# Experts sorted by their token counts, with a last large block each: 512 tokens for four experts and 448 for the other four

## The chip, the cores and the metric

The kernel runs on one core of a Trainium2 chip. The metric is the device time of one execution in microseconds (us); a version's time is the median of its runs. The core's engines are TensorE (PE in the profile; PEld is its weight loads), VectorE (DVE), ScalarE (ACT), GpSimd (POOL) and SyncE (SP), each with an instruction queue of its own, beside the DMA engines.

## The reference

Two parts run one after the other, all in float32. First an attention without softmax over 8 batches of 2496 tokens; then each token goes through the two-layer network of one of eight experts, which is chosen by a hash of the token's id.

```python
# u, v: (8, 2496, 256); z: (8, 2496, 64)
scores = (1.0 / S) * np.matmul(z, z.transpose(0, 2, 1))
attn = np.maximum(scores, 0.0) ** 2
x = (u * np.matmul(attn, v)).reshape(19968, 256)
# w1: (8, 256, 1024); w2: (8, 1024, 256)
expert_idx = token_ids * 2654435761 % 8
for e in range(8):
    mask = expert_idx == e
    out[mask] = np.maximum(x[mask] @ w1[e], 0.0) @ w2[e]
```

The multiplier is 1 modulo 8, so a token's expert is the low three bits of its id. How many tokens an expert gets depends on the ids alone; the kernel learns it only while it runs, so the program must hold for any distribution.

## The kernel before

**Attention.** 200 steps, one for each batch, group of 256 queries (per half of the sequence) and group of keys. TensorE makes scores (L251), ScalarE applies the relu and the square, VectorE forms sums and differences (L275 to L278), and TensorE multiplies them with v in seven products in place of eight (L326). The last query group of a half has 224 queries, so its matmuls have 224 columns. The order of all instructions is written out by hand.

**Routing.** The generator `places()` (from L433) computes, while the attention runs, the slot of each token in a DRAM buffer `x_slots`. The attention's loop calls it once in each step of the list ROUTE, up to its next `yield`; when it has ended, the gated rows of the attention are scattered to their slots by indirect DMAs of POOL (`sort`, L411), and the slots' token numbers are entered into a table (`enter`, L662). Inside `places()`:

- each token's expert (`eid`), a mask of 8 experts by 160 columns, and the number of tokens of each expert;
- a relabelling: the expert with the most tokens becomes label 0, by an exclusive or with its number (`most_i`), so that the others change places in pairs (L513 to L530);
- ranks by matmuls with triangular and full matrices and a scan (L543 to L550);
- `share()` (L560 on): a number of blocks for each label, by a shift of its count, a running sum, and a clamp of the sum at the number of blocks that there are;
- two levels, large blocks of 512 and small blocks of 128. A label gets a further large block if over 128 tokens are left. What doesn't fit goes to small blocks;
- zeros written by indirect DMAs into the last large and the last small block of each label (L653), and the expert of each block (`eb_i`), to be read by SP when it loads weights;
- the slot of each token, from its rank plus an offset by level (L630 to L650).

**Experts.** 40 large blocks (NL) of 512 tokens follow, five for each expert, one after another in the order of their slots. For a block, `load_x` fetches x in a layout that VectorE turns by transposes of 32 by 32 (`turn_x`, L753); `load_w` reads the expert's number from `eb_i` and fetches weights of 1.75 MB for each of the two layers, prepared beforehand as seven factors (`w_blocks`); `up_big` and `down_big` multiply, seven products in place of eight, with half a block's tokens (256) as the columns of each matmul (L972, L1011); the outputs are turned back through DRAM (L1027, L1029) and scattered to the output's rows (`store`, L924). The last large block takes `down_last`, which has the tokens as rows of the result. Up-projections, down-projections and transposes of neighbouring blocks are interleaved by the strings ORDER.

One small block (SMALLS = 1) is unrolled beside the last large block: `up_small` (L1067), `down_small` (L1078). Any further small blocks run in a loop at the very end (L1130), whose number of passes, `n_others`, is read from SBUF when the program gets there:

```python
    n_others = nc.values_load(others_i[0:1, 0:1], min_val=0, max_val=NR - SMALLS)
    with tc.For_i(0, n_others, 1) as n:
```

A pass reads the block's expert, loads both layers' weights (1 MB each), 128 tokens' x and 128 row numbers (`to`), turns x, does 16 and 8 matmuls in the source (32 and 16 instructions, since each float32 matmul is two in the trace), and scatters 128 rows.

Of the kernel before, what the change touches and what calls it, by code (L numbers as in the profile page):

```python
# [12 lines left out]
I32 = mybir.dt.int32  # L13
# [11 lines left out]
def kernel(  # L25
# [31 lines left out]
    NL = E * -(-N // (E * BLK))  # L57
    SMALLS = 1
    NR = max(E, (N - (NL - E) * BLK - E * (P + 1) + E * (P - 1)) // P)
# [361 lines left out]

# [10 lines left out]
    def places():  # L432

        with tc.tile_pool(name="route", bufs=1) as route:
# [15 lines left out]
            zero = route.tile([P, TB * D], F32)  # L450
# [13 lines left out]
            row_of = route.tile([P, 2], F32)  # L464
            nc.gpsimd.iota(row_of[:], pattern=[[NL * BLK, 2]], base=0, channel_multiplier=1,
                           allow_small_or_imprecise_dtypes=True)

            unused = list(range((NL - E) * TB, NL * TB + SMALLS, 7))

            def fill():  # L470
                if unused:
                    c = unused.pop(0)
                    n = min(7, NL * TB + SMALLS - c)
                    nc.sync.dma_start(
                        x_dram[ds(c * P, n * P), :].rearrange("(c p) d -> p c d", p=P), zero[:, 0:D].unsqueeze(1).to_broadcast([P, n, D]))
# [13 lines left out]

            def masks():  # L490
                c = 2 * (B - 1) * T
                nc.vector.tensor_copy(eid[:, 0:c], eid_i[:, 0:2 * (B - 1)].rearrange("p b t -> p (b t)"))
                for ts_ in (slice(0, 2 * LATE), slice(2 * LATE, T)):
                    n = ts_.stop - ts_.start
                    nc.vector.tensor_copy(eid[:, c:c + 2 * n].rearrange("p (b t) -> p b t", b=2), eid_i[:, 2 * (B - 1):, ts_])
                    c += 2 * n
                nc.vector.tensor_tensor(
                    mask[:], eid[:].unsqueeze(1).to_broadcast([P, E, C]),
                    iota_e[:].unsqueeze(2).to_broadcast([P, E, C]), op=OP.is_equal)
# [3 lines left out]
            yield  # L503

# [11 lines left out]
            most = route.tile([P, 1], F32)  # L516
            nc.vector.tensor_reduce(most[:], total[:], axis=AX.X, op=OP.max)
            nc.vector.tensor_scalar(total[:], total[:], most[:], float(-E), op0=OP.is_ge, op1=OP.mult)
            nc.vector.tensor_add(total[:], total[:], iota_e[:])
            nc.vector.tensor_reduce(most[:], total[:], axis=AX.X, op=OP.min)  # L520
            most_i = route.tile([P, 1], I32)
            nc.vector.tensor_copy(most_i[:], most[:])
# [3 lines left out]
            for n, cols in columns:  # L526
                x = eid_i[0:n, :, cols]
                nc.vector.tensor_tensor(x, x, most_i[0:n].unsqueeze(2).to_broadcast(list(x.shape)), op=OP.bitwise_xor)
                nc.vector.tensor_scalar(x, x, E - 1, None, op0=OP.bitwise_and)
# [45 lines left out]
            levels, base, added, unfilled = [], 0, None, []  # L575
            for size, spare, limit, name in ((BLK, BLK - P - 1, NL, "large"), (P, P - 1, NR, "small")):
                n, end = share(count, size, spare, limit, name)
                if limit == NL:
                    yield
                more = route.tile([P, E], F32, name=name + "_more")  # L580
                nc.vector.tensor_sub(more[:], end[:], n[:])
                nc.vector.tensor_scalar(more[:], more[:], float(size), float(base), op0=OP.mult, op1=OP.add)
                nc.vector.tensor_sub(more[:], more[:], first[:])
                total_more = route.tile([P, E], F32, name=name + "_total")
                nc.vector.tensor_copy(total_more[:], more[:])
                if added is not None:
                    nc.vector.tensor_sub(more[:], more[:], added[:])
                added = total_more
                levels.append((first, more, end))
                taken = route.tile([P, E], F32, name=name + "_taken")  # L590
                nc.vector.tensor_scalar(taken[:], n[:], float(size), None, op0=OP.mult)
                nc.vector.tensor_sub(count[:], count[:], taken[:])


                last = route.tile([P, E], F32, name=name + "_last")
                rows_i = route.tile([P, E], I32, name=name + "_rows")
                nc.vector.tensor_scalar(last[:], end[:], -1.0, 0.0, op0=OP.add, op1=OP.max)
                which = int(limit == NR)
                nc.vector.tensor_scalar(rows_i[:], last[:], float(P), row_of[:, which:which + 1], op0=OP.mult, op1=OP.add)
                unfilled += [(rows_i[:, e:e + 1], size // P) for e in range(E)]  # L600
                if limit != NR:
                    nc.vector.tensor_scalar(count[:], count[:], 0.0, None, op0=OP.max)
                    next_first = route.tile([P, E], F32, name=name + "_first")
                    nc.vector.tensor_add(next_first[:], first[:], taken[:])
                    first = next_first
                base += limit * size
                yield
# [3 lines left out]
            for (_, _, end), b0, nb in zip(levels, (0, NL), (NL, NR)):  # L611
                over = upto[0:1].rearrange(flat_e)[:, 0:nb * E].rearrange('p (j e) -> p j e', e=E)
                nc.vector.tensor_tensor(
                    over, end[0:1, :].unsqueeze(1).to_broadcast([1, nb, E]),
                    iota_b[:, 0:nb].unsqueeze(2).to_broadcast([1, nb, E]), op=OP.is_le)
                eb = route.tile([1, max(NL, NR)], F32, name="eb")
                nc.vector.tensor_reduce(eb[:, 0:nb], over, axis=AX.X, op=OP.add)
                nc.vector.tensor_scalar(eb_i[:, b0:b0 + nb], eb[:, 0:nb], float(E - 1), None, op0=OP.min)
                if nb == NL:
                    yield  # L620
            nc.vector.tensor_scalar(others_i[:], levels[1][2][0:1, E - 1:E], float(-SMALLS), 0.0, op0=OP.add, op1=OP.max)
            nc.vector.tensor_tensor(eb_i[:], eb_i[:], most_i[0:1].to_broadcast([1, NB]), op=OP.bitwise_xor)
            nc.vector.tensor_scalar(eb_i[:], eb_i[:], E - 1, None, op0=OP.bitwise_and)

# [4 lines left out]
            lowest, more, _ = levels[1]  # L629
            nc.vector.tensor_tensor(upto, rank[:], each(lowest), op=OP.is_ge)  # L630
            yield
            nc.vector.tensor_mul(upto, upto, each(more))
            for k in range(0, len(unfilled), 4):
                yield
                for rows, n in unfilled[k:k + 4]:
                    zeros(rows, zero, n)
            nc.vector.tensor_add(rank[:], rank[:], each(levels[0][1]))
            yield
            nc.vector.tensor_add(rank[:], rank[:], upto)
            yield  # L640
# [11 lines left out]
    def zeros(rows, zero, n):  # L652
        nc.gpsimd.indirect_dma_start(  # L653
            out=x_dram.rearrange("(r n) d -> r (n d)", n=n), out_offset=bass.IndirectOffsetOnAxis(ap=rows, axis=0),
            in_=zero[:, 0:n * D], in_offset=None, bounds_check=NS * P // n - 1, oob_is_err=False)
# [76 lines left out]

    def half(j):
        return len(slot_tiles(j)) * P // 2

    def load_x(j):
        n = len(slot_tiles(j)) * P
# [184 lines left out]
    def store(j, t, o):  # L922
        col = slot_tiles(j)[t]
        st = nc.gpsimd.indirect_dma_start(  # L924
            out=out[:], out_offset=bass.IndirectOffsetOnAxis(ap=idx[:, col:col + 1], axis=0),
            in_=o, in_offset=None, bounds_check=N - 1, oob_is_err=False)
# [75 lines left out]
    def down_big(j):  # L1002


        take, banks = down_factors(j), {}

        def made(m, _):
            ps, first = down_bank(m, banks)
            x, k = take[m]
            for f in range(FQ):  # L1010
                nc.tensor.matmul(ps[:], w2_block(w2[j], k)[:, f], x[:, f], start=first and f == 0, stop=f == FQ - 1, skip_group_check=True)  # L1011
            return ps[:]
        r = rpool.tile([P, 2, 2 * P], F32, name="ro")
        o = rpool.tile([P, 2, 2, 2 * P], F32, name="oT")
# [3 lines left out]
        def done(x, i, k, ps=None):  # L1018
            if ps is not None:
                nc.scalar.copy(x, ps)  # L1020
            elif i != k:
                for k in range(2):
                    nc.vector.transpose(y[:, ts(i, BLK // L // 2), :, k], o[:, k, i].rearrange("p (j r) -> p j r", r=L))
        yield from products(made, r[:, 0], r[:, 1], c(0, 0), c(0, 1), c(1, 0), c(1, 1), done)
        rows = nc.dram_tensor(f"o_{j}", (BLK, D), F32)
        for q in range(P // L):
            nc.gpsimd.dma_start(out=rows.rearrange("(j r) (q e) -> q r j e", r=L, q=P // L)[q], in_=y[ts(q, L)].rearrange("r j d k -> r j (d k)"))  # L1027
        y = rpool.tile([P, TB, D], F32, name="o_sb", bufs=1)
        nc.gpsimd.dma_start(out=y[:], in_=rows.rearrange("(t p) d -> p t d", p=P))  # L1029
# [61 lines left out]
    BIG, SMALL = list(range(NL)), [[]] * (NL - 1) + [list(range(NL, NL + SMALLS))]  # L1091
    assert SMALLS == 1
# [94 lines left out]
```

## Time and profile before

| | |
|---|---|
| median of 3 runs | 2441.69 us (2438.97 to 2443.9) |
| profiled execution | 2438.23 us |
| its span in the profile | 2436.4 us |
| mean granted TensorE clock | 0.998 |
| TensorE busy | 2416.5 us, 99% |
| VectorE, ScalarE, POOL busy | 1817.1, 728.1, 707.9 us |
| DMA | 559.59 MB, mean 230 GB/s |

In the lines of the profile, a group of instructions is given by its line in the kernel, engine, operation, output and inputs, shape and number; busy time in all and the mean of one in ns follow. In the timeline each line has the start and the duration in us and then the same names, with "x8" for eight instructions drawn together; what stands in brackets is idle time before and what ended it. A line of waits says who waited for whom, the total, how many times, and the longest. A line of windows gives a stretch, its length, the busy time of PE, PEld, DVE, ACT and POOL, the granted clock of TensorE, the DMA engines' busy share and GB/s.

Matmuls are pipelined, so the distance between the starts of two of them, not the duration of one, says what a matmul takes of TensorE's time.

### The profile page before, as it was taken

How to read it: one execution, taken by the hardware profiler on the slowest of the kernel's cores; microseconds unless marked ns; L12 is line 12 of the kernel's file. 1: busy time of each engine (PE TensorE's matmuls, PEld its weight loads, DVE VectorE, ACT ScalarE, POOL GpSimd, SP SyncE). 2: the span in 40 equal slices, each digit the busy share in tenths (PEclk: the TensorE clock that was granted, in tenths of full speed). 3: DMA queues.
4: the chain of work that ended last, by engine and by line, in shares of the span. 5: the costliest groups of instructions: out<-in, count | busy, mean ns of one | idle time of the engine just before them, and what ended most of it. 6: DMA issues, size and time to landing. Idle time of an engine off the chain costs nothing. (4 is left out here: it accounts for less than half of the span.)

```text
span 2436.4 us, 32657 instructions
## 1 busy us (share of the span) xinstructions
PE 2416.5 (99%) x11167; PEld 2010.0 (82%) x11167; DVE 1817.1 (75%) x3811; ACT 728.1 (30%) x1210; POOL 707.9 (29%) x742
## 2 busy tenths in 40 slices
PE   8999999999999999999999999999999999999998
PEld 6787787787787787787787788888888888888887
DVE  7778778868869769768778667777777777777774
ACT  4324314314324224224224212222222222222221
POOL 0002013433434424513411121333233323232323
PEclk9999999999999999999999999999999999999999
DMA  7766667888888888778778677777767776867683
GB/s 151 200 204 190 154 199 230 243 274 257 240 265 254 254 258 255 243 215 249 247 220 257 187 236 230 224 255 222 260 213 265 216 259 218 259 217 258 223 270 117
DMA packets 425193, 559.59 MB, mean 230 GB/s; under 512 B 257372, under 2 KB 350381, under 8 KB 406592
## 3 DMA queue, kind: packets, MB, share of 16 engines
q1 hardware_dynamic: 350704, 326.23, 47.6%
q0 software_dynamic: 41872, 133.39, 15.6%
q10 hardware_dynamic: 32448, 97.86, 12.1%
q8 instruction: 88, 1.44, 0.2%
q14 instruction: 81, 0.66, 0.1%
HBM read 353.28 MB, written 200.26 MB: 227 GB/s over the span
## 5 line engine op out<-in xcount | busy, mean ns | idle before, releaser
L255 ACT ACTIVATE a<-s_ps 128x512 f32<-128x512 f32 (+1 forms) x480 | 246.2, 599 | 699.2 <-PE s_ps L251 601.3
L326 PE MATMUL acc<-t,vc 128*128 128x256 f32 (+3 forms) x1600 | 402.2, 373 | 0.0
L326 PEld LDWEIGHTS acc<-a,v_sb 128*128 128x128 f32 (+1 forms) x1600 | 293.2, 190 | 119.1 <-issue 56.5
L411 POOL DMA_INDIRECT x_slots<-x_row,row x160 | 193.5, 1209 | 680.4 <-DVE x_row L389 558.4
L326 PE MATMUL acc<-a,v_sb 128*128 128x256 f32 (+3 forms) x1600 | 382.7, 382 | 0.1
L326 PE MATMUL acc<-t,v_sb 128*128 128x256 f32 (+3 forms) x1600 | 369.7, 373 | 0.0
L326 PEld LDWEIGHTS acc<-t,vc 128*128 128x128 f32 (+1 forms) x1600 | 303.5, 190 | 33.6
L326 PEld LDWEIGHTS acc<-t,v_sb 128*128 128x128 f32 (+1 forms) x1600 | 303.4, 190 | 33.6
L972 PE MATMUL h_ps<-xs,w 128*128 128x256 f32 x1280 | 316.0, 380 | 0.0
L1011 PE MATMUL o_ps<-h,w 128*128 128x256 f32 x1248 | 294.8, 379 | 0.0
L275 DVE TENSOR_TENSOR t<-a 128x512 f32<-128x512 f32 (+1 forms) x200 | 134.2, 671 | 203.9 <-ACT a L264 144.7
L979 ACT ACTIVATE h<-h 128x512 f32<-128x512 f32 x240 | 151.1, 630 | 418.6 <-DVE h L942 176.9
L972 PEld LDWEIGHTS h_ps<-xs,w 128*128 128x128 f32 x1280 | 243.6, 190 | 32.4
L1011 PEld LDWEIGHTS o_ps<-h,w 128*128 128x128 f32 x1248 | 243.1, 195 | 27.2
L251 PE MATMUL s_ps<-zT 64*128 64x512 f32 (+1 forms) x960 | 240.2, 616 | 7.8 <-DVE zT L186 7.8
L972 PE MATMUL h_ps<-xT,w 128*128 128x256 f32 x960 | 234.7, 380 | 2.5 <-DVE h L942 2.5
L1011 PE MATMUL o_ps<-hs,w 128*128 128x256 f32 x936 | 221.1, 379 | 0.0
L291 DVE STREAM_TRANSPOSE mirror<-a 128x256 f32<-128x256 f32 x640 | 217.8, 407 | 2.0 <-DMA scores<-mirror 1.8
L924 POOL DMA_INDIRECT out_dram<-o_sb,idx x156 | 159.3, 1021 | 187.4 <-DMA o_sb<-o 151.7
L662 POOL DMA_INDIRECT slot_tokens<-token,addr x160 | 171.1, 1069 | 134.7 <-DVE addr L650 86.3
L972 PEld LDWEIGHTS h_ps<-xT,w 128*128 128x128 f32 x960 | 182.7, 191 | 27.4 <-DVE h L942 2.9
L326 PE MATMUL acc<-a,vc 128*128 128x256 f32 (+3 forms) x800 | 201.1, 373 | 0.0
(182 smaller groups left out, 2610.1 us busy)
## 6 DMA issues: line engine op xcount, KB each, us to landing
w<-w_blocks SPq DMA_DIRECT2D x80, 1792.0 KB
scores<-mirror SPq DMA_DIRECT2D x192, 256.0 KB
a<-scores ACTq DMA_DIRECT2D x48, 1024.0 KB
scores<-mirror SPq DMA_DIRECT2D x224, 128.0 KB
a<-scores ACTq DMA_DIRECT2D x32, 896.0 KB
w_blocks<-w POOLq DMA_DIRECT2D x16, 1792.0 KB
xq<-x_slots SPq DMA_DIRECT2D x160, 128.0 KB
o<-y POOLq DMA_DIRECT2D x156, 128.0 KB
```

The lines of the kernel that those rows point to most:

```text
L251: nc.tensor.matmul(flat(ps)[:, 0:2 * w].rearrange("p (q c) -> p q c", q=2), tile_of_keys(b, h, s, j), q_h, start=True, stop=True)
L255: nc.scalar.activation(of[:, :, j, h].rearrange("p m q e -> p q m e"), flat(ps)[:, 0:2 * w].rearrange("p (q m e) -> p q m e", q=2, e=in_bl ...
L275: nc.vector.tensor_sub(t1, y12, y11)
L291: nc.vector.transpose(to, in_blocks(a, g)[:, :, j, h].rearrange("p i q (r t) -> p t i q r", t=2)[:, t])
L326: nc.tensor.matmul(acc[k][:, half, 0:w], x[0:n, j, :], y[0:n, j], start=(first and j == 0 and half == 0), stop=(last and j == 1), skip_gro ...
L411: st = nc.gpsimd.indirect_dma_start(out=x_dram[:, :], out_offset=bass.IndirectOffsetOnAxis(ap=row[0:m, c:c + 1], axis=0), in_=x_sb[0:m, q, ...
L662: st = nc.gpsimd.indirect_dma_start(out=slot_dram[:, None], out_offset=bass.IndirectOffsetOnAxis(ap=addr[0:n, to:to + 1], axis=0), in_=tok ...
L924: st = nc.gpsimd.indirect_dma_start(out=out[:], out_offset=bass.IndirectOffsetOnAxis(ap=idx[:, col:col + 1], axis=0), in_=o, in_offset=Non ...
L972: nc.tensor.matmul(ps[:, r], w1[j][:, k, ts(f + r, P)], y, start=first and r == 0, stop=True, skip_group_check=True)
L979: lambda o, i, k, ps=None: nc.scalar.activation(o, o if ps is None else ps, AF.Relu))
L1011: nc.tensor.matmul(ps[:], w2_block(w2[j], k)[:, f], x[:, f], start=first and f == 0, stop=f == FQ - 1, skip_group_check=True)
```

## The change

There are still 40 large blocks, but the first 32 (FULL) are shared out as full blocks, and the other eight are one "last" block for each label. The labels are now the experts' places in the order of their counts, the most first: each expert's label is the number of experts with more tokens. The last blocks of labels 0 to 3 hold up to 512 tokens, those of labels 4 to 7 up to 448. What is left beyond the last block goes to small blocks, of which there are now up to 28 in place of 27.

```diff
-    NL = E * -(-N // (E * BLK))
+    LASTS = (BLK,) * (E // 2) + (BLK - 2 * L,) * (E // 2)
+    FULL = E * (N // (E * BLK))
+    NL = FULL + E
     SMALLS = 1
-    NR = max(E, (N - (NL - E) * BLK - E * (P + 1) + E * (P - 1)) // P)
+    NR = max(E, -(-(N - FULL * BLK) // P))
```

The relabelling is a comparison of all pairs of counts, and the tokens' labels are read off the mask:

```diff
-            nc.vector.tensor_reduce(most[:], total[:], axis=AX.X, op=OP.max)
...
+            nc.vector.scalar_tensor_tensor(total[:], total[:], float(E), iota_e[:], op0=OP.mult, op1=OP.subtract)
+            nc.vector.tensor_tensor(pairs[:], *a_b(total[:], total[:]), op=OP.is_lt)
+            nc.vector.tensor_reduce(label[:], pairs[:], axis=AX.X, op=OP.add)
...
+            nc.vector.tensor_tensor(mask[:], mask[:], label[:].unsqueeze(2).to_broadcast([P, E, C]), op=OP.mult)
+            yield
+            labels = route.tile([P, C], F32)
+            nc.vector.tensor_reduce(labels[:], mask[:].rearrange("p e c -> p c e"), axis=AX.X, op=OP.add)
+            nc.vector.tensor_scalar(eid[:], eid[:], float(E), float(E), op0=OP.is_ge, op1=OP.mult)
+            nc.vector.tensor_add(eid[:], eid[:], labels[:])
             masks()
```

The levels become three. The shift of the large level now has no allowance (it was 383, so that over 128 left tokens made a block), and its clamp is FULL; `size_of` holds LASTS:

```diff
-            for size, spare, limit, name in ((BLK, BLK - P - 1, NL, "large"), (P, P - 1, NR, "small")):
+            for size, spare, limit, name in ((BLK, 0, FULL, "large"), (P, P - 1, NR, "small")):
+                if limit == NR:
+                    more = route.tile([P, E], F32, name="last_more")
+                    nc.vector.tensor_scalar(more[:], iota_e[:], float(BLK), float(FULL * BLK), op0=OP.mult, op1=OP.add)
+                    level(more)
+                    taken = route.tile([P, E], F32, name="last_taken")
+                    nc.vector.tensor_tensor(taken[:], count[:], size_of[:], op=OP.min)
+                    nc.vector.tensor_sub(count[:], count[:], taken[:])
...
                 n, end = share(count, size, spare, limit, name)
...
-            nc.vector.tensor_tensor(upto, rank[:], each(lowest), op=OP.is_ge)
-            yield
-            nc.vector.tensor_mul(upto, upto, each(more))
...
+            for k in (1, 2):
+                nc.vector.tensor_tensor(upto, rank[:], each(levels[k][0]), op=OP.is_ge)
+                yield
+                nc.vector.tensor_mul(upto, upto, each(levels[k][1]))
+                for e in range(4 * k - 4, 4 * k):
+                    zeros(rows_i[:, e:e + 1], zero)
+                yield
+                nc.vector.tensor_add(rank[:], rank[:], upto)
+                yield
```

The experts of the blocks (`eb_i`) are looked up from the labels by a comparison and a sum over eight. The indirect writes of zeros are now for small blocks alone, eight in place of sixteen; all last blocks are still zeroed beforehand by `fill()`. `places()` has 29 yields in place of 25.

In the expert part a block's matmuls, sums, loads and stores follow its number of tokens, and the last blocks are put among the full ones, the fewest tokens' first:

```diff
+    def tokens(j):
+        return BLK if j < FULL else LASTS[j - FULL] if big(j) else P
+
     def half(j):
-        return len(slot_tiles(j)) * P // 2
+        return tokens(j) // 2
...
-        nc.gpsimd.dma_start(out=y[:], in_=rows.rearrange("(t p) d -> p t d", p=P))
+        whole, rest = divmod(2 * n, P)
+        nc.gpsimd.dma_start(out=y[:, 0:whole], in_=rows[0:whole * P].rearrange("(t p) d -> p t d", p=P))
+        if rest:
+            nc.gpsimd.dma_start(out=y[0:rest, whole], in_=rows[whole * P:2 * n])
...
-    BIG, SMALL = list(range(NL)), [[]] * (NL - 1) + [list(range(NL, NL + SMALLS))]
+    BIG, SMALL = [x for e in range(E) for x in (*range(e * FULL // E, (e + 1) * FULL // E), NL - 1 - e)], [[]] * (NL - 1) + [list(range(NL, NL + SMALLS))]
```

The last large block of the order, which takes `down_last`, is that of label 0. The loop at the end is unchanged.

## The prediction

> **What bounds the kernel now.** I read the page first, then the waits, then the two stretches the change touches: a large expert block, and the end.
>
> ```profile
> span 2436.4 us, 32657 instructions
> ...
> PE 2416.5 (99%) x11167; PEld 2010.0 (82%) x11167; DVE 1817.1 (75%) x3811; ACT 728.1 (30%) x1210; POOL 707.9 (29%) x742
> ```
>
> ```profile
> PE s_ps L251 <- DVE zT L186: 7.8, 2, 6.9
> PE h_ps L972 <- DVE h L942: 2.5, 1, 2.5
> PE o_ps L1043 <- DVE ro L936: 0.6, 1, 0.6
> ```
>
> The three lines below the page's are all that TensorE (PE) waits for: 10.9 us. So the time is the number of matmuls times their spacing, plus a short tail. Only two things can matter: columns taken out of matmuls, and work put where TensorE no longer covers it.
>
> **How many blocks of which kind.** This is exact, from the inputs: with seed 0, token id modulo 8 gives the experts 2506, 2446, 2582, 2478, 2498, 2473, 2434 and 2551 tokens. Before, an expert takes a further large block if over 128 tokens are left; that makes 5 for each, 40 in all, and 22 tokens of the largest expert go to one small block. That one is unrolled (SMALLS = 1), so the loop at L1130 runs zero times. The trace agrees: 32 matmuls at L1067 are one small block.
>
> After, the full blocks are count // 512, running sum clamped to FULL = 32. In sorted order (2582, 2551, 2506, 2498, 2478, 2473, 2446, 2434) that is 5, 4, 4, 4, 4, 4, 4, 4 = 33, so the clamp leaves the last expert 3. The largest then has 22 tokens left, for which it occupies a "last" block of 512. The smallest has 2434 − 1536 = 898 left; its last block takes 448, and 450 remain: four small blocks. One is unrolled, **three go through the loop at the end**, which has no other work beside it.
>
> **Gain: four blocks of 448.** A 448-token block issues the same matmuls with 224 columns in place of 256. The attention part already runs both widths, in two stretches of 28 matmuls of equal make:
>
> ```profile
> 323.07 1.89 PE L326 MATMUL acc<-a,v_sb 128*128 128x256 f32 x8
> ...
> 329.11 1.90 PE L326 MATMUL acc<-a,v_sb 128*128 128x256 f32 x8
> ...
> 348.42 1.68 PE L326 MATMUL acc<-a,v_sb 128*128 128x224 f32 x8
> ...
> 353.72 1.68 PE L326 MATMUL acc<-a,v_sb 128*128 128x224 f32 x8
> ```
>
> The starts give 6.04 us / 28 = 0.2157 us at 256 columns and 5.30 / 28 = 0.1893 at 224. A block has (1280 + 960) / 40 = 56 matmul instructions up and 56 down: 112 × 0.2157 = 24.16 us, and the weight issues of SyncE (SP) below come 24.17 apart, so a block is matmul spacing and nothing else. Saved: 112 × 0.0264 = 2.96 us per block, **11.8 us** for four. VectorE is busy 691 of 964 us in these blocks (17.3 us per block), fits into the 21.2 us that remain, and shrinks too. The next block's transfers keep the DMA engines near 9 tenths for some 4.5 slices of 3.9 us, 17.7 us in each 24.17, and fit as well: their slack is 6.5 us a block, above the 2.96 that go.
>
> ```profile
> 2310.15 1.59 SPq L769 DMA_DIRECT2D w<-w_blocks  x2
> ...
> 2334.33 1.49 SPq L769 DMA_DIRECT2D w<-w_blocks  x2
> ```
>
> **Cost: three passes of the loop.** A pass loads 2 MB of weights and 128 KB of x, turns x, computes, and stores, one after the other: the weight tiles are single (bufs=1), and TensorE has nothing else. Its rows:
>
> ```profile
> 2359.80 0.41 SPq L772 DMA_DIRECT2D w1s<-in_moe_w_dram  x1
> 2361.01 21.13 SPq L769 DMA_DIRECT2D w<-w_blocks  x2
> ...
> 2383.34 1.95 PE L1067 MATMUL h_ps<-xTs,w1s 128*128 128x128 f32 x16
> ...
> 2416.67 0.78 POOL L1029 DMA_DIRECT2D o_sb<-o  x1 [2.90 <-issue]
> ...
> 2421.03 1.04 POOL L924 DMA_INDIRECT out_dram<-o_sb,idx  x1 [3.57 <-DMA o_sb<-o]
> ...
> 2424.04 3.62 PE L1078 MATMUL o_ps<-w2s,h 128*128 128x256 f32 x16
> ...
> 2431.36 0.97 POOL L924 DMA_INDIRECT out_dram<-o,idx  x1 [0.30 <-issue]
> ```
>
> - Loading, issue: 1.3 us from one weight load to the next on SP (2359.80 to 2361.01, and its register read).
> - Loading, transfer: 2.23 MB. Quickest: 424 GB/s, the best slice of the DMA view from 2280 to 2437 us, 5.3 us. Dearest: the 512 KB of o_sb landed 4.36 us after its issue began; less 0.78 of issue and 1.85 of landing that is 1.8 us, or 295 GB/s, hence 7.6 us. I take 6.4. Landing: 1.85 us, from the end of the last store's issue (2432.33) to SP's last semaphore of L1130 (2434.2). x is issued behind both weights, so TensorE waits for all of it.
> - Turning x: 0.44 (the one transpose of xTs) and a hand-over, 0.5 us.
> - Computing: up 2 × (1.95 + 0.68 for the relu), in turn since they share one PSUM tile; down 3.62; copy 0.37; some 0.9, an estimate, for the hand-overs (from the down matmuls' end, 2427.66, to ScalarE's copy, 2428.14, is 0.48; I count it as about two of them): 10.2 us.
> - Storing: 0.97 of issue and 1.85 of landing, 2.8 us.
> - From pass to pass: the engines must meet. At zero passes they already do, once; L1130's semaphores and branches end on SP at 2434.2 and on PE at 2434.8, 0.6 us. The program's end, which drains, clears semaphores and meets twice, takes 1.9 us (L1182, 2434.4 to 2436.3). I take 1.9, the nearer in kind.
> - TensorE's clock. It idles some 15 us in each pass, and the last matmul here ended at 2427.7:
>
> ```profile
> 2428.00:2429.00 1.00, 0.00 (x0) 0.00 (x0) 0.00 (x0) 0.37 (x1) 0.69 (x2) 1.00 0.11 37
> 2429.00:2430.00 1.00, 0.00 (x0) 0.00 (x0) 0.00 (x0) 0.00 (x0) 0.77 (x1) 0.88 0.44 148
> 2430.00:2432.00 2.00, 0.00 (x0) 0.00 (x0) 0.00 (x0) 0.00 (x0) 1.62 (x2) 0.50 0.27 91
> ```
>
> The column before the last two is the granted clock: 1.00, then 0.88, then 0.50, so it halves about 2 us after the last matmul and each pass starts at half. Half all the way doubles the streaming, 2 × 1.8 + 3.45 = 7 us (16 × 0.113 twice, 16 × 0.2157); recovery at once costs 0. The trace shows no recovery; I take the middle, 3.5.
>
> A pass: 1.3 + 6.4 + 1.85 + 0.5 + 10.2 + 2.8 + 1.9 + 3.5 = **28.4 us**; with the low ends of transfer, meeting and clock 22.5, with the high ends 33.1. Three: **85 us**, between 67 and 99.
>
> The Trainium skill, "TensorE: Matmul & The Clock Gate", Part 1, says that the clock falls to half after an idle window of about 3.4 us and returns after some 3.4 us of sustained work. The fall agrees with the row above; the return no row here shows. By it the first 3.4 us of matmuls run at half speed, an estimate of 1.7 us per pass in place of 3.5, and three passes would cost 80 us.
>
> **What costs nothing.** Routing grows by some 10 us of VectorE in steps of 0.2 to 2.3 us: two more passes over 1280 elements for the labels (1.49 as L497, 2.33 as L645), three more over rank (1.45 each, as L630 to L637), and small ones. From 320 to 600 us VectorE idles 57 of 280 while TensorE idles 0.02; that slack hides it. Uncovered it is 10 us; I put 0, and 10 into the range. Four more yields end routing some five steps (of about 7 us) later; sorting starts then, and its backlog of one more group is worked off by the seven fetches per 25 steps, against five made. Eight indirect zero fills go from POOL (about 1.1 us each, 9 us off a queue at 29%). A 448 block adds one POOL issue (0.78 us) ahead of its stores, hidden under 21 us of matmuls. The new order moves no load past another: every block fetched its own weights already.
>
> **Sum** against the profiled execution (2438.2 us, span 2436.4): 2438.2 − 11.8 + 85.2 = 2511.6. The median of the runs shown (2441.7) is 3.5 above that execution, so on its scale **2515 us**.
>
> **Rivals.**
> - *Three passes as above*, 22.5 to 33.1 us each: 2497 to 2529. Chance 0.72.
> - *Dearer passes*, 34 to 42 us: the loop body's instructions, which no engine has run here, arrive late (the page lists instruction transfers, q8 and q14), or 128 scattered 4-byte reads (`to`) land last. For it: nothing in the trace shows the body. Against: every piece of it has a row. 2532 to 2556. Chance 0.12.
> - *Cheaper passes*, 17 to 22.5 us: the next pass's weights start while the last one stores (2.8 + 1.9 us hidden), and the clock recovers at once. Against: L1130 has every engine meet. 2481 to 2497. Chance 0.12.
> - *No pass, faster*: the fifth full block of the largest expert doesn't displace one of the smallest, so that only the 448-blocks tell: 2441.7 − 11.8 = 2430. It decides from a largest expert under 2560 tokens on, or a pass under 11.8 / 3 = 3.9 us; but its matmuls alone stream for 7 us, and 2582 is counted. Chance 0.04: it is also the case that I misread the sharing.
>
> **The numbers.** The range 2487 to 2540 reaches from the middle of the cheaper case through the likeliest with 10 us for routing, into the dearer one. The measurement tells 0.2% (5 us) from no change: faster 0.04, same 0.01, slower 0.95.
>
> **What would show it.** three times the 32 + 16 matmuls of a small block, on the loop's own lines, in the final 85 us; matmuls of 128x224 in the expert part at 0.189 us spacing; blocks 21.2 us apart four times; the granted clock at 0.5 when each pass starts; TensorE idle before the loop still about 11 us. It would be wrong if the loop ran another number of times, or if TensorE waits appeared in attention, where routing grew.

## The result and the profile after

The changed kernel takes 2511.16 us (median of 4 runs, 2507.2 to 2517.55); the kernel before, measured beside it, 2442.8. The ratio is 1.0285, with a 95% interval of 1.0269 to 1.0301: slower, 4 us under the predicted 2515. The profiled execution took 2513.03 us, with a span of 2511.2, 74.8 more than before.

The page, with the same rows as those shown of before:

```profile
span 2511.2 us, 33192 instructions
...
PE 2441.9 (97%) x11311; PEld 2038.4 (81%) x11311; DVE 1825.3 (73%) x3824; ACT 727.1 (29%) x1213; POOL 707.1 (28%) x749
```

TensorE has 144 instructions more: three times 32 + 16, three passes of the loop. Its share falls from 99% to 97%: it now waits. What it waited for:

```profile
PE h_ps L1190 <- DVE xTs L1184: 33.2, 2, 17.3
PE h_ps L1190 <- issue: 9.0, 1, 9.0
PE s_ps L254 <- DVE zT L189: 8.0, 2, 7.0
PE s_ps L254 <- DMA zT<-zT: 4.1, 1, 4.1
...
PE acc L329 <- DVE o L342: 1.8, 1, 1.8
```

The first two are the loop's passes (L1190 is its up-projection) and were forecast. The third was there before. The last two lie in the attention, are new, and were not forecast; the prediction had named waits in the attention as a sign that it would be wrong.

**The blocks of 448.** SP's timeline, where each line is the weight issue of one block:

```profile
1640.37 1.50 SPq L803 DMA_DIRECT2D w<-w_blocks  x2
1664.54 1.85 SPq L803 DMA_DIRECT2D w<-w_blocks  x2
1687.22 1.50 SPq L803 DMA_DIRECT2D w<-w_blocks  x2
1709.90 1.50 SPq L803 DMA_DIRECT2D w<-w_blocks  x2
1734.07 1.50 SPq L803 DMA_DIRECT2D w<-w_blocks  x2
```

24.17, then 22.68 twice, then 24.17 again. A block's down-projection runs among its successor's up-projection, so one short block shortens two distances by 1.49 us each. To see where the 74.8 us came from I compared when ScalarE does the same copy (`oT`, one per block but the last) in the two traces. Before and after, each line with the starts of the first and the last of these copies:

```profile
L1020 ACT COPY oT<-o_ps x39: 372/372/373, 1477.9 to 2402.7; 128x256 f32<-128x256 f32 x39
```

```profile
L1057 ACT COPY oT<-o_ps x39: 345/372/372, 1488.0 to 2400.8; 128x256 f32<-128x256 f32 x35, 128x224 f32<-128x224 f32 x4
```

By the timelines the first is 10.05 us late against before (1487.96 and 1477.91), the last 1.90 early (2400.76 and 2402.66): the four blocks gave back **11.95 us**, and the attention had lost **10.05**. The rest of the span, behind the last of these copies, is 76.7 us longer.

**The passes.** Timeline, from the unrolled tail to the second pass:

```profile
2388.66 0.40 SPq L1174 DMA_DIRECT2D w1s<-in_moe_w_dram  x1
...
2426.72 0.37 SPq L1176 DMA_DIRECT2D w2s<-in_moe_w_dram  x1
...
2428.12 3.61 SPq L1180 DMA_DIRECT2D xqs<-x_slots  x4
...
2429.84 0.97 POOL L959 DMA_INDIRECT out_dram<-o,idx  x1 [0.31 <-issue]
...
2434.78 3.76 PE L1190 MATMUL h_ps<-xTs,w1s 128*128 128x128 f32 x16 [9.01 <-issue]
...
2449.38 0.37 ACT L1196 COPY o<-o_ps 128x256 f32<-128x256 f32 x1 [22.28 <-PE o_ps L1194]
2450.03 0.97 POOL L1197 DMA_INDIRECT out_dram<-o,to  x1 [19.21 <-ACT o L1196]
2456.68 0.40 SPq L1174 DMA_DIRECT2D w1s<-in_moe_w_dram  x1
...
2466.66 3.76 PE L1190 MATMUL h_ps<-xTs,w1s 128*128 128x128 f32 x16 [17.32 <-DVE xTs L1184]
```

SP issues the first layer's weights of the first pass at 2388.66, 41 us before the last unrolled store: it goes into the loop ahead of the other engines. Only these weights are that early. For those of the second layer SP waits 34.2 us, until the unrolled small block's down-projection is done with their buffer, and x is issued behind them, while the unrolled stores still run. The trace of the kernel before, whose loop runs zero times, has SP at the loop's line ahead of TensorE too (first and last start; PEld is TensorE's queue here):

```profile
L1130 SPq COMPARE_BRANCH  x3: 38/38/62, 2383.4 to 2434.2; - x3
L1130 PEldq COMPARE_BRANCH  x3: 101/179/336, 2424.6 to 2434.8; - x3
```

In the second pass the weights are issued only when the pass before has stored (SP waits 19.4 us for it), and it is 10 us from their issue to the first matmul. Sixteen up-projection instructions take 3.76 us; in the unrolled block they took 1.95. The windows say why (the column before the last two is the granted clock):

```profile
2434.00:2436.00 2.00, 1.22 (x6) 1.25 (x7) 0.45 (x1) 0.00 (x0) 0.00 (x0) 0.50 0.00 0
...
2446.00:2448.00 2.00, 2.00 (x7) 1.60 (x7) 0.00 (x0) 0.00 (x0) 0.00 (x0) 0.64 0.00 0
2448.00:2450.00 2.00, 1.34 (x7) 0.84 (x5) 0.00 (x0) 0.37 (x1) 0.00 (x0) 1.00 0.00 0
```

The clock is at half for the first 12.7 us of the pass (to 2447.43 in the trace). From the first matmul to the end of ScalarE's copy the three passes take 15.0, 13.2 and 11.4 us.

**The attention.** Two places. VectorE's timeline around the first:

```profile
121.11 2.32 DVE L541 TENSOR_REDUCE labels<-mask 128x160 f32<-128x1280 bf16 x1
...
123.97 1.49 DVE L504 TENSOR_TENSOR mask<-eid,iota_e 128x1280 bf16<-128x1280 f32 x1
...
129.96 0.37 DVE L342 TENSOR_TENSOR o<-r,acc 128x256 f32<-128x256 f32 x1
```

Labels and masks, 4.4 us in one step, stand ahead of the join of a finished query group (L342 and on), which has to free the accumulators; TensorE waits 1.8 us for it, and the attention's steps are 2.15 us late from there on. The second place is SP's queue near 730 us. Before:

```profile
726.08 0.58 SPq L372 DMA_DIRECT2D x_row<-x  x1
726.76 0.99 SPq L223 DMA_DIRECT2D u_sb<-in_u_dram  x2
727.85 0.47 SPq L193 DMA_DIRECT2D zT<-zT  x1
```

And after:

```profile
729.51 2.38 SPq L379 DMA_DIRECT2D x_row<-x  x2
732.08 0.90 SPq L226 DMA_DIRECT2D u_sb<-in_u_dram  x2
733.07 0.47 SPq L196 DMA_DIRECT2D zT<-zT  x1
```

Since routing ends five steps later, another group is due to be fetched here, one whose x comes in two transfers, and the copy of z for the next batch is issued 5.2 us later, of which 2.8 are the steps' own lateness by then. It landed only when TensorE, at 740.83, had waited 4.1 us; the clock had gone to half and came back near 747.6 (0.69, 0.50, 0.50 and 0.60 in the four windows of 2 us from 740 on). Together 8.4 us: 4.1 of waiting, some 3.4 from 6.8 us at half clock, and 0.9 that I did not place.

### The profile page after: what moved, and what is told of

It is laid out like the page before. It is cut to its first block, busy times and chain, and to the rows that moved or that the text cites. A ratio compares the mean times of both kernels' runs of the same rounds, so it can differ in the third digit from the quotient of the medians.

```text
span 2511.2 us, 33192 instructions
## 1 busy us (share of the span) xinstructions
PE 2441.9 (97%) x11311; PEld 2038.4 (81%) x11311; DVE 1825.3 (73%) x3824; ACT 727.1 (29%) x1213; POOL 707.1 (28%) x749
## 3 DMA queue, kind: packets, MB, share of 16 engines
q10 hardware_dynamic: 32448, 97.86, 11.8%
## 5 line engine op out<-in xcount | busy, mean ns | idle before, releaser
L1007 PE MATMUL h_ps<-xs,w 128*128 128x256 f32 (+1 forms) x1280 | 311.9, 376 | 0.0
L1048 PE MATMUL o_ps<-h,w 128*128 128x256 f32 (+1 forms) x1248 | 291.4, 376 | 0.0
L1014 ACT ACTIVATE h<-h 128x512 f32<-128x512 f32 (+1 forms) x240 | 149.9, 625 | 413.0 <-DVE h L977 176.3
L1007 PE MATMUL h_ps<-xT,w 128*128 128x256 f32 (+1 forms) x960 | 231.4, 377 | 2.7 <-DVE h L977 2.7
L1048 PE MATMUL o_ps<-hs,w 128*128 128x256 f32 (+1 forms) x936 | 218.6, 376 | 0.0
```

The lines of the kernel that those rows point to most:

```text
L1007: nc.tensor.matmul(ps[:, r], w1[j][:, k, ts(f + r, P)], y, start=first and r == 0, stop=True, skip_group_check=True)
L1014: lambda o, i, k, ps=None: nc.scalar.activation(o, o if ps is None else ps, AF.Relu))
L1048: nc.tensor.matmul(ps, w2_block(w2[j], k)[:, f], x[:, f], start=first and f == 0, stop=f == FQ - 1, skip_group_check=True)
```

## The experiments

**At most four full blocks.** With this, the largest expert doesn't displace a block of the smallest:

```diff
-                nc.vector.tensor_copy(n[:], n_i[:])
+                if limit == FULL:
+                    nc.vector.tensor_scalar(n[:], n_i[:], float(FULL // E), None, op0=OP.min)
+                else:
+                    nc.vector.tensor_copy(n[:], n_i[:])
```

> Each expert gets at most four full blocks, so that one small block remains and the loop runs zero times; nothing else changes (right for inputs in which each expert has at least 2048 tokens, as here). Theory: by the two traces the three passes hold 76.7 us of the span, the attention is 10.05 us longer and the four blocks of 448 give 11.95 back; without passes about 1.9 us under before, some 2441 us (ratio 0.999). Rival, the prediction's own terms (passes 85 us, nothing lost in attention): 2426 to 2431 us (ratio 0.995). Rival, the new order or the last blocks cost something that the passes hide: above 2446 us.

2434.73 us (before beside it 2439.65; ratio 0.9977, 0.9966 to 0.9988). The passes are gone, and they were the whole loss. The expected 2441 was too high by 6: 3 of them are the level of the kernel before, which ran at 2442.8 beside the changed kernel; besides, I had put the 10.05 us of one execution's attention into the sum. Here the attention is 6.0 us late (its one wait for a z copy, 1.2 us, ends at 557.6, in an earlier batch), and the runs scatter from 2432 to 2441. That the attention's loss isn't a fixed amount was the first thing this showed.

**Without blocks of 448**, on top of that:

```diff
-    LASTS = (BLK,) * (E // 2) + (BLK - 2 * L,) * (E // 2)
+    LASTS = (BLK,) * E
```

> As the run with at most four full blocks, and all last blocks at 512, so that no block has 448: sorting, levels and order alone. Theory: 10.05 us above before, 2453 us, and 11.95 us above the run with at most four; the distance between the expert part's blocks is 24.17 us throughout. Rival (448 saves less, attention loses less): 2443 to 2447 us.

2447.92 us, ratio 1.0034 (1.0022 to 1.0045): 8.3 above the kernel before beside it, where 10.05 was expected, and 13.2 above the run with 448, where 11.95 was; its attention is 8.65 us late in the trace, against 6.0. By the ScalarE copies nothing is gained from the first block to the last (8.65 late at both), where every kernel with 448 gains 11.95. So the blocks' term is settled, and sorting, levels and order alone make the kernel slower.

**One pass in place of three:**

```diff
-            nc.vector.tensor_scalar(others_i[:], ends[1][0:1, E - 1:E], float(-SMALLS), 0.0, op0=OP.add, op1=OP.max)
+            nc.vector.tensor_scalar(others_i[:], ends[1][0:1, E - 1:E], float(-SMALLS - 2), 0.0, op0=OP.add, op1=OP.max)
```

> The changed kernel with one pass of the loop in place of three; the last two small blocks (194 tokens) are left out. Theory: the first pass begins its loads under the unrolled tail and costs 19.8 us (from 2434.5, where the span would end without passes, to 4.3 us behind its store's start at 2450.0), so about 2461 us, and the other two 28.4 each. Rival: every pass costs the same 25.6 us, 2466.5 us.

2448.98 us, 14.3 above the run without passes, neither value. In the trace the attention is 1.4 us late, against 6.0 in the other, so the pair can't be set against each other by medians; by stages the time behind the last block's copy is 22.1 us longer than before, and 2.3 longer in the run without passes, which makes 19.8 for the pass, as the theory had it. I repeated it later with a steady attention.

**Matmuls while loading**, in each pass:

```diff
+        idle = up_ps.tile([P, 2, 2 * P], F32, name="h_ps", tag="other")
+        for _ in range(36):
+            nc.tensor.matmul(idle[:, 0, 0:P], ident[:], ident[:], start=True, stop=True)
```

> The changed kernel, and in each pass 36 matmuls of the identity with itself (72 instructions) whose results nobody reads, issued while the pass loads, to keep TensorE busy. Theory: the half clock costs 4.8, 3.0 and 1.2 us in the three passes of the profile; if the extra matmuls bring the full clock back before the data land, about 2502 us, with some 10.2 us of computing per pass. Rival: the clock stays at half in them too, they take 16 us and end after the data have landed: 2518 us or more. Rival: the clock has no share in it: 2511 us.

2495.03 us, ratio 1.0226 (1.0207 to 1.0246), 16 under the changed kernel and 7 under what I expected. The second pass:

```profile
2442.91 10.61 PE L1185 MATMUL h_ps<-ident 128*128 128x128 f32 x72 [6.47 <-PEq L1171]
...
2453.59 2.02 PE L1193 MATMUL h_ps<-xTs,w1s 128*128 128x128 f32 x16
...
2459.23 3.72 PE L1197 MATMUL o_ps<-w2s,h 128*128 128x256 f32 x16 [0.78 <-DVE h L1194]
2462.99 0.37 ACT L1199 COPY o<-o_ps 128x256 f32<-128x256 f32 x1 [26.13 <-PE o_ps L1197]
```

and its windows:

```profile
2446.00:2448.00 2.00, 2.00 (x12) 2.00 (x11) 0.00 (x0) 0.00 (x0) 0.00 (x0) 0.55 0.99 407
2448.00:2450.00 2.00, 2.00 (x20) 2.00 (x19) 0.00 (x0) 0.00 (x0) 0.00 (x0) 1.00 1.07 370
```

Adding useless work to TensorE makes the kernel faster: the clock is back before the data are, and the pass computes in 9.8 us (2453.59 to 2463.36), all three in 29.3 in place of 39.5. That is 10.2 us for the half clock, 9.0 expected; the time behind the last block is 65.2 us longer than before, in place of 76.7, 11.5 less. The two profiled executions are 18.0 us apart; the other 6.5 are the attention, 3.6 us late here and 10.05 there.

**The fetch behind the z copy**, with at most four full blocks:

```diff
-    FETCH = (1, 5, 8, 12, 15, 19, 22)
+    FETCH = (1, 5, 8, 12, 15, 19, 23)
```

> At most four full blocks, and the last of the seven fetch steps of a batch is 23 in place of 22, so that SP issues this fetch behind the z copy of step 23 and no longer ahead of it. Theory: the 4.1 us wait of TensorE for the z copy and the half clock after it (together 8.4 us in the profile of the changed kernel) come from SP's queue: about 8.4 us under the run with at most four, some 2432.5 us. Rival: the copy lands late because the DMA engines are full, or the wait was of that one execution: no change, 2441 us.

2432.21 us (2429.63 to 2433.14), ratio 0.9962 (0.9949 to 0.9976). No wait for the copy is left:

```profile
PE s_ps L254 <- DVE zT L189: 8.0, 2, 7.0
PE h_ps L1010 <- DVE h L980: 2.5, 1, 2.5
PE acc L329 <- DVE o L342: 1.8, 1, 1.8
PE o_ps L1086 <- DVE ro L974: 0.6, 1, 0.6
```

But the median fell by 2.5 us (with the kernel before beside it 1.1 higher), not by 8.4. What did fall is the scatter, from 9.6 us (12 runs) to 3.5 (5 runs): the wait comes in some executions and not in others. The traces of the runs with one pass and with matmuls while loading agree: they have the old fetch step and no wait for a z copy.

**And the labels in a step of their own:**

```diff
             nc.vector.tensor_add(eid[:], eid[:], labels[:])
+            yield
             masks()
```

> As the run with the later fetch, and one more yield between the labels and the masks, so that the 4.4 us of VectorE in one step become 2.9 and 1.5 in two. Theory: the 2.15 us that the attention lost at that step go too: some 2430 us, 12 us under before. Rival: routing's VectorE work shows wherever it is put, or the further step of delay brings another wait: 2432.5 us or more.

2428.97 us (2428.24 to 2430.65), before beside it 2440.71: ratio **0.9951** (0.9938 to 0.9965). 3.2 us less, where 2.15 were expected; the wait for the join shrinks to 0.7 us and the attention is as long as before (0.13 us early at the first block's copy), with all of routing's added VectorE work still in it. This version beats both kernels. It is right only where every expert has at least 2048 tokens; a general one would have to hand on full blocks that a smaller expert can't fill.

**The kernel before, with its routing as late as the changed one's:**

```diff
             for _ in range(2):
                 yield
                 fill()
-            yield
+            for _ in range(5):
+                yield
```

> The kernel before, with four empty yields more early in routing, so that routing ends at the step at which the changed kernel's does; no work is added. Theory: the delay alone (one group more of backlog to fetch) puts a longer fetch ahead of the z copy: 8.4 us above before, 2451 us, with TensorE waiting some 4 us for the z copy near 730 us. Rival: it is routing's added VectorE work that does it: as before, 2443 us.

2440.41 us, ratio 0.9991 (0.9981 to 1.0001): as before. The theory that the delay costs 8.4 us each time falls. Yet the profiled execution, 2447.64 us, shows that wait, 3.1 us, and an attention 9.4 us late, with no work added:

```profile
PE s_ps L251 <- DMA zT<-zT: 3.1, 1, 3.1
```

So the event needs none of the change's work, and the delay doesn't make it the rule. Does the kernel before have it too? Its runs beside this kernel reach from 2438.96 to 2450.51.

**The kernel before, with the fetch behind the z copy** (the same line of FETCH):

> The kernel before, with the last fetch step of a batch at 23 in place of 22 and nothing else. Theory: executions of the kernel before that come out at 2445 to 2450 us are those in which TensorE waits for the z copy and its clock halves; with the fetch behind the copy these go, the runs lie within 4 us of each other, and the median falls by 0 to 2 us to some 2439. Rival: the scatter of the kernel before has another cause: still 10 us between the runs.

2438.88 us; the 11 runs lie between 2437.15 and 2440.86, while 6 of the 21 runs of the kernel before beside it lie above 2443. By median the ratio is 0.9992 (0.9983 to 1.0002), not told from no change; no late execution is left. 6 of 21 against 0 of 11 would come by chance about once in seventeen, so the kernel before probably has the event as well, in a quarter to a third of its executions. None of its late executions was profiled: the wait itself is not shown in it.

**Three passes, and one, with a steady attention.** Both take the changed kernel with the later fetch and the further yield; the second has one pass:

> The changed kernel with its three passes, the later fetch and the further yield between labels and masks, that is, the run with both of these and without the limit of four full blocks. Theory: the three passes cost 74 to 77 us beside the 2429 us of that run: 2503 to 2506 us. Rival, the prediction's 28.4 us per pass: 2514 us.

> As the run before it, with one pass in place of three (the last two small blocks, 194 tokens, are left out). Theory: the first pass costs 19.8 to 22 us, 2449 to 2451 us, and the other two 27.3 each. Rival, all passes alike: a third of the three passes' price, 25.6 us, 2454.6 us; or, as the medians of the earlier pair had it, 14.3 us, 2443 us.

2502.06 us and 2446.62 us (before beside them 2440.33), against 2428.97 with none (before 2440.71). Three passes cost 73.1 us, 1 us under the expected span; the first costs 17.7, and each of the others (73.1 − 17.7) / 2 = 27.7. With one pass the median is 2.4 us under the expected 2449. In the traces, behind the last block's copy, the three passes hold 74.2 us more than the run without any, and the one pass 20.6 (its profiled execution is the slowest of its 11), which leaves 26.8 for each of the others. By both ways the first pass is the cheapest and all alike (24.4) does not hold; whether it costs 18 or 21 us is not settled.

## Why the prediction was right, step by step

- **Three passes, from the counts**: right, 96 up-projection instructions at L1190. The passes are the loss: without them the changed kernel is not slower.
- **The blocks of 448**: 11.8 us forecast, 11.95 measured. Only the picture was off, eight distances of 22.68 us in place of four of 21.2.
- **The passes' size**: 85.2 us forecast, 73.1 by the runs (76.7 in the profiled execution). Passes 2 and 3 were right, 27.7 us each against 28.4. The term that was mis-sized is the first pass's loading: I took the meeting of the engines as standing between the tail and the loop, and put 9.6 us of loading into all three. SP reads the number of passes on its own and issues the first layer's weights 41 us ahead, and the other loads while the tail's last stores run: TensorE stood idle for 9.0 us ahead of the first pass, and for 17.3 and 15.9 ahead of the others. The first pass costs 17.7 us by the runs. The rows of L1130 in the kernel before, which I had read only at their ends, already had SP there 41 us ahead of TensorE. (A slip that changes little: 4.36 less 0.78 and 1.85 is 1.73 us, not 1.8, so the dearest transfer is 7.4 us and not 7.6.)
- **The half clock**: 3.5 us per pass taken as the middle between 0 and 7; 10.2 us in three, 3.4 each. That the middle fits is luck: the passes are at half for 12.7, 8.1 and 3.4 us of their matmuls. The clause of the prediction on the Trainium skill ("TensorE: Matmul & The Clock Gate", Part 1: the full clock returns after some 3.4 us of sustained work) gave an estimate of 1.7. Unbroken work comes near the page's figure: in the run with matmuls while loading the clock is back 4.9 and 3.6 us after they begin (2442.91 to 2447.79, 2468.12 to 2471.68). The passes' own matmuls are not unbroken, they stop twice for the relu (0.78 us each), and for two of the three passes the estimate was too low.
- **When the clock changes**: the granted clock of the trace changes only at multiples of 3.41 us (it is at half for 17.07, 20.48 and 17.07 us around the three passes). Cut into stretches of this length, the first pass fills them with matmuls to 71, 77, 77 and 100%, the second to 37, 77 and 100%, the third to 98%, and each time the clock is back at the end of the last of these. So a burst of 3.8 us that lies across two stretches need not bring it back. That the filling decides was not tested, and one stretch speaks against so plain a rule: behind the wait in the attention, matmuls fill the one up to 744.18 to 98%, and the clock is back only one later, at 747.60. The prediction also took the fall to agree with the same page's idle window of about 3.4 us. But its row has the half clock from 2429.76 on, 2.1 us after the last matmul, and the same trace has a fall at the end of a wait of only 2.5 us (L972, clock at half from 1460.38 to 1463.79). That place shows a return too, after 3.4 us of matmuls; the prediction had not looked for one.
- **Routing at nothing**: wrong in the profiled execution, by the 10.05 us that I had put aside as the price without cover, but not in that way. VectorE got 9.7 us more, as forecast (some 10); the idle share that I showed is a mean from 320 to 600 us, while routing's VectorE work runs from 84 to 329 us in the kernel before (to 360 in the changed one), and a mean says nothing of a step in which 4.4 us stand ahead of a join. That cost 3.2 us by the runs. The other part isn't VectorE's at all: the backlog that I had called worked off changed which fetch stands ahead of a z copy. I had counted the fetches and not looked at what is queued behind one of them on SP. With this the prediction's own sign of being wrong came about, TensorE waits in the attention: 17.2 us of waiting outside the loop, where it said about 11.
- **The sum**: 2515 against 2511. That it comes so close is luck: two misses cancel, 8 to 12 us too much for the passes and some 6 to 10 too little for the attention. By the runs: −11.95 + 73.1 + 3.2 (labels) + 2.5 (z copy, in the mean) = +66.9, from medians of different rounds; measured 68.4.

Left open: why the z copy takes 7.8 us to land in one execution and 4.4 in another (the run with at most four full blocks); the DMA engines' share is 0.83 and 1.03 in the two windows from 734 to 738 us, but that this is the cause was not tried. And with the limit of four full blocks the program's end, behind the last block, is 2.3 us longer in the profiles than in the kernel before. The traces place it behind the loop, in POOL's DRAIN instruction: 3.34 us against 0.89. Why that takes longer is open.

## What to carry to other kernels

A clamp on a running sum takes from whoever comes last: before asking what a smaller block saves, count with the real inputs what spills, and where it runs; here 12 us of saved columns bought 73 us of uncovered work. Work added in the shade of a busy engine is paid by the step, not by the mean: look at what stands behind it in that step, and on each queue that its delay reorders. And where a total comes out right, check the terms: here the first pass and the attention did not.

## What was not expected of the hardware

- Useless matmuls made the loop 11.5 us quicker (76.7 to 65.2 us behind the last block, against before): TensorE's clock, at half after each wait for loads, was back before they landed.
- In an engine kept at 99%, a single wait of 4.1 us cost 8.4: the clock had halved by the end of the wait and stayed so for 6.8 us of matmuls behind it. In the kernel before a wait of 2.5 us was enough to halve it for 3.4 us.
- An engine runs into a dynamic loop ahead of the others as far as its own waits let it: SP issued the first layer's weights of the first pass 41 us before the last store ahead of the loop.
